# When the first weights of a fused attention and two-layer kernel are begun, and where their VectorE steps write

## Chip, cores and metric

One Trainium2 chip, one core. The metric is the device time of one execution in microseconds.

## The reference

Attention with a decay per head over blocks of 64, then a gated layer and a layer with a maximum of three, all in fp32:

```python
intra = np.einsum('bhic,bhjc->bhij', qb, kb) * Dmask[None]          # per block of 64
intra = np.einsum('bhij,bhjd->bhid', intra, vb)
inter = np.einsum('bhid,bhde->bhie', qb * lam_pow[None], kv_state)
out[:, :, sl] = intra + inter
kv_state = lam_block[None, :, None, None] * kv_state + np.einsum('bhsd,bhse->bhde', kb_dec, vb)
...
rms = np.sqrt(np.mean(x * x, axis=-1, keepdims=True) + 1e-06)       # x: 1536 x 512
xn = x / rms * rms_g
g = xn @ w_gate                                                     # d_ff 1536
silu = g * (1.0 / (1.0 + np.exp(-g)))
x = silu * (xn @ w_val) @ w_out
...
h = np.maximum(np.maximum(x @ w1, x @ w2), x @ w3)                  # d_ff 768
return h @ w_out
```

q, k and v are 2 x 8 heads x 768 x 64.

## The kernel before

Tokens are worked on as twelve tiles of 128 rows (index c), and the layers take them as three blocks of 512 (four tiles each). Each fp32 matrix product is made of three matmuls in fp32r on high and low halves (L466 to L468): a weight comes as `wh` and `wl`, an activation as `xh` and `xl`.

**Attention in rounds.** The attention of a tile is cut into pieces, named by letters in `named` (L428): T turns q and k (loads for two tiles ahead are asked for first), K makes the decayed keys `kd` on GpSimd, C the scores on TensorE, a and b mask the two halves (a also advances the state), V advances the state again, M mixes and squares, U sums the squares into `ms` and takes `ri` on GpSimd, N normalises (`x` on VectorE, `xh` on ScalarE), R makes `xl` (on GpSimd for the first eight tiles). The list `attn_q` (L430) holds the order of the pieces: round s works T on tile s, C, a, b and V on s - 1, M and U on s - 2, N and R on s - 3, and K on s + 1. Each engine runs its instructions in the order in which they are written. From tile 4 on M also reduces the squares on VectorE, so that U has one slice to sum and not four (L388 to L400).

**The seven rounds ahead of the projections** (L968) run the attention of the first tiles: rounds 0 to 6. After round 6 the first block is there, and `first_stage` begins: four steps per block, each of 24 projection matmuls (pg, then pv) and later 12 for the output, with a `gap` after every six. In the gaps of the first four steps (24 of them) the pieces of rounds 7 to 10 are placed, and in every second one `make_unit`.

**A weight** (a unit, 128 x 512) passes through stations: `load_to` asks for it on SyncE's queue (three buffers, `wraw`); `begin_unit` has ScalarE split it into words (L238, L239); `words_of_unit` has three VectorE steps (n = 0, 1, 2: L196, L199, L202) and an addition on GpSimd (L204), which also frees the `wraw` buffer; `finish_unit` casts `wh` on ScalarE (L167) and subtracts `wl` on GpSimd (L170). `make_unit` finishes the weight that has its words, does the words of the next, and begins a third. The flag `narrow` says where the middle result of the three steps lies: in the SBUF tile `W` itself while it is true, in a bank of PSUM (`mid`) when it is false. There are eight banks, which every product and every `mid` takes in turn; a new tile waits until the last reader of its bank is through.

In the seven rounds a weight is loaded at the end of each of rounds 2, 3 and 4, two at the end of rounds 5 and 6, and `make_unit` runs at the end of rounds 3 to 6. So the first weight's words are made after round 4, the second's after round 5, the third's after round 6.

Of the kernel before, what the change touches and what calls it, by code (L numbers as in the profile page):

```python
# [26 lines left out]
def tile_decay_attention_swiglu_maxout(  # L27
# [30 lines left out]
    NCH = NT // P  # L58
    CPNB = NB // P
# [35 lines left out]
    def loads_to(c):  # L95
        while nxt_load[0] <= min(c, NCH):
            n = nxt_load[0]
            if n:
                load(n - 1, 2)
            if n < NCH:  # L100
                load(n, 0)
                load(n, 1)
            nxt_load[0] += 1
# [40 lines left out]
    stage1, stage2 = [], []  # L144
# [5 lines left out]
    pos = {"load": 0, "made": 0, "raw": 0, "step": 0, "gap": 0, "quiet": False, "lag": 3, "narrow": True, "seam": False}  # L150
# [176 lines left out]
    def masked(hf):  # L327
        def piece(c):
            d = st[c]
            nc.vector.tensor_tensor(  # L330
                out=d["A"].rearrange("p (a t) i -> p t a i", t=2)[:, hf],
                in0=d["sc"][hf][:, :HF].rearrange("p (a i) -> p a i", i=C),
                in1=Tm.rearrange("p (a t) i -> p t a i", t=2)[:, hf], op=ALU.mult)
            if hf == 0:
                d["S0"] = last_state[0]
                d["S1"] = next_state(c, 0, d["S0"])
        return piece
# [40 lines left out]
    def mixed(c):  # L378
        for part in range(2):
            half_mixed(c, part)  # L380
        px = st[c]["px"]
        sq = att.tile([P, NP, P], F32, tag="sq", name="sq", bufs=1)
        x = att.tile([P, NP, P], F32, tag="x", name="x", bufs=3)
        for n in range(2):
            nc.scalar.activation(out=sq[:, 2 * n:2 * n + 2, :], in_=px[n][:, :2, :], func=AF.Square)
        for a in range(NP):
            nc.scalar.activation(out=x[:, a, :], in_=px[a // 2][:, a % 2, :], func=AF.Copy, scale=g_sb[:, a:a + 1])
        ss = sq  # L388
        if c >= CPNB:
            ss = att.tile([P, 1, P], F32, tag="ss", name="ss", bufs=1)  # L390
            nc.vector.tensor_reduce(out=ss[:, 0, :], in_=sq.rearrange("p a t -> p t a"),
                                    axis=mybir.AxisListType.X, op=ALU.add)
        st[c] = dict(x=x, ss=ss)
# [26 lines left out]
    def rest(c):  # L420
# [5 lines left out]
        eng.tensor_tensor(out=bl[:, :, ts], in0=x, in1=bh[:, :, ts].bitcast(F32), op=ALU.subtract)  # L426

    named = dict(M=(2, mixed), N=(3, normed), C=(1, scores), a=(1, masked(0)), R=(3, rest),  # L428
                 b=(1, masked(1)), U=(2, summed), V=(1, advance), T=(0, lambda c: (loads_to(c + 2), turn(c))), K=(-1, decayed_keys))
    attn_q = [(s_, named[ch][1], s_ - named[ch][0]) for s_ in range(NCH + 3)  # L430
              for ch in ("MCaNbTURVK" if s_ <= CPNB + 2 else "MNCaUbVTKR") if (ch == "K") <= s_ - named[ch][0] < NCH]
    gaps = [0, 0]

    def attn_step():
        _, fn, c = attn_q.pop(0)
        fn(c)
# [505 lines left out]
    with tc.manual_schedule():  # L942
        nc.scalar.dma_start(out=lam8, in_=lam.rearrange("(o h) -> o h", o=1).to_broadcast([P, H]))
        loads_to(0)
        for to, src in crosswise(g_sb, rms_g.rearrange("(a p) -> p a", p=P)):
            nc.scalar.dma_start(out=to, in_=src)
        make_identity(nc, ident)
        nc.vector.memset(ones, 1.0)
        nc.vector.memset(zeros, 0.0)
        nc.scalar.activation(out=mhalf, in_=zeros[:, 0:1], func=AF.Silu)  # L950
        nc.vector.memset(mhalf, -0.5)
        warm = bank("warm")
        for i in range(9):
            nc.tensor.matmul(out=warm[:, 0:P], lhsT=zeros, rhs=zeros, start=True, stop=True)
        nc.vector.tensor_tensor(out=diag, in0=ident[:, :C], in1=ident[:, C:], op=ALU.add)
        for h in range(H):
            nc.vector.tensor_tensor_scan(
                out=Tm[:, h, :], data0=lam8[:, h:h + 1].to_broadcast([P, C]), data1=diag,
                initial=0.0, op0=ALU.mult, op1=ALU.add)
        for hf in range(2):  # L960
            nc.vector.tensor_copy(out=lamh[64 * hf:64 * hf + 64, :],
                                  in_=lam8.rearrange("p (a t) -> p t a", t=2)[64 * hf:64 * hf + 64, hf, :])
        for a in range(NP):
            nc.vector.tensor_tensor_scan(
                out=lami[:, a, :], data0=lamh[:, a:a + 1].to_broadcast([P, C]), data1=zeros[:, :C],
                initial=1.0, op0=ALU.mult, op1=ALU.add)
        loads_to(1)
        for s_ in range(CPNB + 3):  # L968
            while attn_q[0][0] == s_:
                attn_step()  # L970
            load_to(pos["load"] + (0, 0, 1, 1, 1, 2, 2)[s_])
            if s_ > 2:
                make_unit()
        finish = first_stage()
        pos["step"] = len(steps)
        second_stage(finish)
# [31 lines left out]
```

## Time and profile before

| | us |
|---|---|
| median of three runs | 562.12 (561.74 to 563.1) |
| profiled execution | 560.44 |
| its span, first to last instruction | 558.6 |
| TensorE busy | 534.4 (96%) |
| VectorE busy | 385.1 (69%) |
| ScalarE busy | 279.0 (50%) |
| GpSimd busy | 317.4 (57%) |

In a timeline row stand the start, the length, the engine, the line, the operation, what is written from what, and in brackets the idle time before it with what ended it. PE is TensorE, DVE VectorE, ACT ScalarE, POOL GpSimd, SPq the DMA queue of SyncE. [...]

### The profile page before, as it was taken

To read this page: it belongs to the slowest core of one execution; us is meant where nothing else is said; L and a number is where in the kernel's file an instruction comes from. 1 tells how busy PE (TensorE), PEld (TensorE's weight loads), DVE (VectorE), ACT (ScalarE), POOL (GpSimd) and SP (SyncE) were. 2 spreads that over 40 slices of the span, in tenths; PEclk is the share of its full clock that TensorE was granted. 3 is DMA by queue.
4 is the path that set the end of the run, shared out by engine and by line. 5 is a ranking of instruction groups with operands and counts; after the bars stand their busy time and mean duration, and the time that the engine had idled before them with its cause. 6 is when DMAs were issued, how large, how long until landed. Compare 5 with 4: busy or idle time off the path is not lost.

```text
span 558.6 us, 9707 instructions
## 1 busy us (share of the span) xinstructions
PE 534.4 (96%) x3716; PEld 439.5 (79%) x3716; DVE 385.1 (69%) x664; ACT 279.0 (50%) x541; POOL 317.4 (57%) x251
## 2 busy tenths in 40 slices
PE   7976988899999999999999999999999999999997
PEld 7864766678888888888888888888888888888885
DVE  6687998363888558566685776877677577684463
ACT  3554755252474676326527445646565756551120
POOL 2366796611599668335726737787386554962050
PEclk9976989999999999999999999999999999999999
DMA  8965646200112223111312222120222322210014
GB/s 194 225 171 133 170 121 166 76 3 1 38 39 75 77 75 114 38 39 38 114 38 76 75 77 76 39 75 1 75 76 76 111 79 63 89 38 1 0 54 172
DMA packets 65453, 44.66 MB, mean 80 GB/s; under 512 B 40064, under 2 KB 61568, under 8 KB 65408
## 3 DMA queue, kind: packets, MB, share of 16 engines
q1 hardware_dynamic: 64704, 44.05, 27.5%
q8 instruction: 29, 0.48, 0.4%
q14 instruction: 16, 0.13, 0.1%
q10 hardware_dynamic: 704, 0.01, 0.1%
HBM read 40.90 MB, written 3.15 MB: 79 GB/s over the span
## 4 chain that ended last, share of the span: by engine, by line
PE 81%; POOL 7%; DVE 4%; DMA 3%; issue 2%; ACT 1%; SPq 1%; POOLq 0%; ACTq 0%; DVEq 0%
PE p L674 33%; PE r L674 8%; PE acc L466 5%; PE acc L468 5%; PE acc L467 5%; PE q L674 4%; PE acc L857 3%; PE acc L858 3%; PE acc L856 3%; POOL W L204 2%; POOL wl L170 2%; PE pv L468 2%; PE pv L466 2%; PE pv L467 1%; PE pg L467 1%
## 5 line engine op out<-in xcount | busy, mean ns | idle before, releaser
L170 POOL TENSOR_TENSOR wl<-W,wh 128x512 fp32r<-128x512 f32 x77 | 105.5, 1370 | 40.8 <-ACT wh L167 40.8
L204 POOL TENSOR_TENSOR W<-W,wraw 128x512 int32<-128x512 int32 x60 | 81.1, 1352 | 82.9 <-DVE W L202 66.2
L167 ACT CAST wh<-W 128x512 fp32r<-128x512 f32 x77 | 47.8, 621 | 92.3 <-POOL W L204 91.8
L480 POOL TENSOR_TENSOR hl<-sg,hh 128x512 fp32r<-128x512 f32 x36 | 48.3, 1341 | 33.8 <-ACT hh L479 33.8
L674 PE MATMUL p<-xh,wh 128*128 128x512 f32 x148 | 57.6, 389 | 0.0
L674 PE MATMUL p<-xl,wh 128*128 128x512 f32 x148 | 57.6, 389 | 0.0
L674 PE MATMUL p<-xh,wl 128*128 128x512 f32 x148 | 57.6, 389 | 0.0
L466 PE MATMUL acc<-hh,wh 128*128 128x512 f32 x144 | 56.6, 393 | 0.0
L467 PE MATMUL acc<-hl,wh 128*128 128x512 f32 x144 | 56.1, 389 | 0.0
L468 PE MATMUL acc<-hh,wl 128*128 128x512 f32 x144 | 56.1, 389 | 0.0
L829 DVE TENSOR_TENSOR acc_sb<-acc,acc_sb 128x512 f32<-128x512 f32 x46 | 31.8, 691 | 21.3 <-PE acc L468 20.2
L238 ACT ACTIVATE W<-wraw 128x512 f32<-128x512 f32 x60 | 40.1, 669 | 8.1 <-DMA wraw<-in_moe_w_dram 3.3
L239 ACT ACTIVATE wraw<-wraw 128x512 int32<-128x512 uint32 x60 | 39.9, 665 | 0.0
L729 ACT COPY c<-p 128x512 f32<-128x512 f32 x34 | 19.9, 586 | 38.0 <-PE p L674 37.8
L480 POOL TENSOR_TENSOR hl<-m,hh 128x512 fp32r<-128x512 f32 x18 | 24.1, 1344 | 23.0 <-ACT hh L479 22.9
L479 ACT CAST hh<-sg 128x512 fp32r<-128x512 f32 x36 | 22.3, 619 | 29.4 <-DVE sg L613 20.8
L674 PE MATMUL p<-yh,wh 128*128 128x512 f32 x90 | 35.0, 389 | 0.0
L674 PE MATMUL p<-yl,wh 128*128 128x512 f32 x90 | 35.0, 389 | 0.0
L674 PE MATMUL p<-yh,wl 128*128 128x512 f32 x90 | 35.0, 389 | 0.0
L196 DVE TENSOR_SCALAR mid<-W 128x512 f32<-128x512 f32 x46 | 31.5, 685 | 3.4 <-ACT W L238 3.4
L199 DVE TENSOR_SCALAR mid<-mid 128x512 int32<-128x512 int32 x46 | 31.9, 694 | 0.7
L674 PEld LDWEIGHTS p<-xl,wh 128*128 128x128 f32 x148 | 27.8, 188 | 5.8
(175 smaller groups left out, 1375.4 us busy)
## 6 DMA issues: line engine op xcount, KB each, us to landing
wraw<-in_moe_w_out_dram SPq DMA_DIRECT2D x18, 512.0 KB, 3.3
wraw<-in_moe_w_dram SPq DMA_DIRECT2D x18, 512.0 KB, 3.5
kn<-in_k_dram SPq DMA_DIRECT2D x12, 256.0 KB, 4.3
qn<-in_q_dram SPq DMA_DIRECT2D x12, 256.0 KB, 4.6
vn<-in_v_dram SPq DMA_DIRECT2D x12, 256.0 KB, 4.0
wraw<-in_moe_w_gate_dram SPq DMA_DIRECT2D x12, 256.0 KB, 2.9
wraw<-in_moe_w_gate_dram SPq DMA_DIRECT2D x24, 128.0 KB, 3.2
wraw<-in_moe_w_val_dram SPq DMA_DIRECT2D x12, 256.0 KB, 2.9
```

The source lines that it names most:

```text
L167: nc.scalar.copy(out=wh, in_=W.bitcast(F32))
L170: nc.gpsimd.tensor_tensor(out=wl, in0=W.bitcast(F32), in1=wh.bitcast(F32), op=ALU.subtract)
L199: nc.vector.tensor_scalar(out=mid[key], in0=mid[key], scalar1=0x07FFFFFF, scalar2=3, op0=ALU.bitwise_and, op1=ALU.logical_shift_left)
L204: nc.gpsimd.tensor_tensor(out=W, in0=W, in1=lo, op=ALU.add)
L238: nc.scalar.activation(out=W.bitcast(F32), in_=hi.bitcast(F32), func=AF.Abs)
L239: nc.scalar.activation(out=lo, in_=lo.bitcast(U32), func=AF.Copy, scale=2.0 ** -29)
L466: nc.tensor.matmul(out=out, lhsT=wh, rhs=xh_, start=first, stop=False)
L467: nc.tensor.matmul(out=out, lhsT=wh, rhs=xl_, start=False, stop=False)
L468: nc.tensor.matmul(out=out, lhsT=wl, rhs=xh_, start=False, stop=last)
L480: nc.gpsimd.tensor_tensor(out=dst_l, in0=src, in1=dst_h.bitcast(F32), op=ALU.subtract)
L674: nc.tensor.matmul(out=ps, lhsT=w[:, ks], rhs=r[:, o + k, :], start=first and k == 0 and n == 0, stop=k == 1 and n == 2, skip_group_check= ...
L829: nc.vector.tensor_tensor(out=ps if kept else y, in0=ps, in1=y, op=ALU.add)
```

## The change

The loop of the seven rounds now places the weights' steps between the attention pieces. A weight is begun at the end of each round from round 2 on, a round earlier than before. In the next round its first step stands after b, its second after U (with the finishing of the weight before it), its third, with GpSimd's addition, after V. `narrow` is false in the loop, so the middle result is a PSUM tile. One weight is asked for at the end of every round from round 0 on, seven in all as before. After the loop three weights are finished where two were, one has its words, and one is begun.

The order of the pieces changes too: in round 6 R stands right after N, ahead of U; from round 7 on it stands right after C instead of at the end. The reduction of the squares begins with tile 5 instead of tile 4.

```diff
--- before.py
+++ after.py
@@ -386,7 +386,7 @@
         for a in range(NP):
             nc.scalar.activation(out=x[:, a, :], in_=px[a // 2][:, a % 2, :], func=AF.Copy, scale=g_sb[:, a:a + 1])
         ss = sq
-        if c >= CPNB:
+        if c > CPNB:
             ss = att.tile([P, 1, P], F32, tag="ss", name="ss", bufs=1)
             nc.vector.tensor_reduce(out=ss[:, 0, :], in_=sq.rearrange("p a t -> p t a"),
                                     axis=mybir.AxisListType.X, op=ALU.add)
@@ -426,9 +426,11 @@
         eng.tensor_tensor(out=bl[:, :, ts], in0=x, in1=bh[:, :, ts].bitcast(F32), op=ALU.subtract)
 
     named = dict(M=(2, mixed), N=(3, normed), C=(1, scores), a=(1, masked(0)), R=(3, rest),
-                 b=(1, masked(1)), U=(2, summed), V=(1, advance), T=(0, lambda c: (loads_to(c + 2), turn(c))), K=(-1, decayed_keys))
-    attn_q = [(s_, named[ch][1], s_ - named[ch][0]) for s_ in range(NCH + 3)
-              for ch in ("MCaNbTURVK" if s_ <= CPNB + 2 else "MNCaUbVTKR") if (ch == "K") <= s_ - named[ch][0] < NCH]
+                 b=(1, masked(1)), U=(2, summed), V=(1, advance), T=(0, lambda c: (loads_to(c + 2), turn(c))),
+                 K=(-1, decayed_keys))
+    orders = ["MCaNbTURVK"] * (CPNB + 2) + ["MCaNRbTUVK"] + ["MNCRaUbVTK"] * NCH
+    attn_q = [(s_, named[ch][1], s_ - named[ch][0]) for s_ in range(NCH + 3) for ch in orders[s_]
+              if (ch == "K") <= s_ - named[ch][0] < NCH]
     gaps = [0, 0]
 
     def attn_step():
@@ -965,12 +967,27 @@
                 out=lami[:, a, :], data0=lamh[:, a:a + 1].to_broadcast([P, C]), data1=zeros[:, :C],
                 initial=1.0, op0=ALU.mult, op1=ALU.add)
         loads_to(1)
+        pos["narrow"] = False
+        unit_ = None
         for s_ in range(CPNB + 3):
+            if stage1:
+                unit_ = stage1.pop(0)
             while attn_q[0][0] == s_:
+                fn = attn_q[0][1]
                 attn_step()
-            load_to(pos["load"] + (0, 0, 1, 1, 1, 2, 2)[s_])
-            if s_ > 2:
-                make_unit()
+                if unit_ and fn is named["b"][1]:
+                    words_of_unit(0, *unit_)
+                elif unit_ and fn is named["U"][1]:
+                    words_of_unit(1, *unit_)
+                    if stage2:
+                        finish_unit(*stage2.pop(0))
+                elif unit_ and fn is named["V"][1]:
+                    words_of_unit(2, *unit_)
+                    stage2.append(unit_[:3])
+            load_to(pos["load"] + 1)
+            if s_ > 1:
+                begin_unit()
+        pos["narrow"] = True
         finish = first_stage()
         pos["step"] = len(steps)
         second_stage(finish)
```

## Rows read from the trace of the kernel before

**Rows 1.** Busy time by engine, four stretches; granted clock, DMA share, GB/s last.

```profile
core 0: us, PE busy (x) PEld busy (x) DVE busy (x) ACT busy (x) POOL busy (x), PEclk, DMA share, GB/s
10.00:30.00 20.00, 18.25 (x561) 16.21 (x561) 14.07 (x48) 12.28 (x34) 7.77 (x9) 1.00 0.97 227
30.00:47.70 17.70, 9.43 (x132) 7.58 (x131) 14.78 (x31) 8.99 (x22) 9.54 (x10) 0.67 0.64 164
47.70:107.70 60.00, 52.45 (x676) 39.97 (x676) 48.74 (x85) 32.41 (x70) 48.54 (x38) 0.93 0.52 138
107.70:558.60 450.90, 446.68 (x2251) 368.82 (x2251) 302.16 (x483) 221.84 (x411) 248.80 (x188) 1.00 0.19 60
```

**Rows 2.** Timeline of TensorE, 40 to 48 us: start, length, instruction, idle before.

```profile
44.27 0.80 PE L466 MATMUL pg<-xh,wh 128*128 128x512 f32 x1 [2.01 <-ACT xh L417]
47.74 0.79 PE L467 MATMUL pg<-xl,wh 128*128 128x512 f32 x1 [2.67 <-POOL xl L426]
```

**Rows 3.** Timeline of GpSimd, 37 to 47 us.

```profile
37.68 1.23 POOL L284 TENSOR_TENSOR kd<-kn,Tm 128x512 f32<-128x512 f32 x1
38.88 1.44 POOL L170 TENSOR_TENSOR wl<-W,wh 128x512 fp32r<-128x512 f32 x1
40.95 1.28 POOL L204 TENSOR_TENSOR W<-W,wraw 128x512 int32<-128x512 int32 x1 [0.63 <-DVE W L202]
45.79 0.75 POOL L404 TENSOR_TENSOR ri<-ms,mhalf 128x1 f32<-128x1 f32 x1 [3.56 <-DMA wraw<-in_moe_w_val_dram]
46.42 1.26 POOL L426 TENSOR_TENSOR xl<-x,xh 128x512 fp32r<-128x512 f32 x1
```

**Rows 4.** Timeline of VectorE, 36 to 43 us.

```profile
36.54 1.47 DVE L196 TENSOR_SCALAR W<-W 128x512 f32<-128x512 f32 x1
...
39.24 1.64 DVE L202 SCALAR_TENSOR_TENSOR W<-wraw,W 128x512 int32<-128x512 int32 x1
40.80 1.02 DVE L391 TENSOR_REDUCE ss<-sq 128x128 f32<-128x512 f32 x1
...
42.84 0.67 DVE L415 TENSOR_TENSOR x<-x,pb 128x512 f32<-128x512 f32 x1
```

**Rows 5.** Timeline of VectorE: steps of other weights, in SBUF.

```profile
28.29 1.48 DVE L196 TENSOR_SCALAR W<-W 128x512 f32<-128x512 f32 x1
...
31.00 0.69 DVE L202 SCALAR_TENSOR_TENSOR W<-wraw,W 128x512 int32<-128x512 int32 x1
...
56.61 0.43 DVE L196 TENSOR_SCALAR W<-W 128x512 f32<-128x512 f32 x1
```

**Rows 6.** Groups of VectorE by shape, 105 to 500 us: count, busy, mean ns.

```profile
L199 DVE TENSOR_SCALAR mid<-mid 128x512 int32<-128x512 int32 x45 | 31.2, 694 | 0.7
L196 DVE TENSOR_SCALAR mid<-W 128x512 f32<-128x512 f32 x45 | 30.8, 685 | 3.4 <-ACT W L238 3.4
L202 DVE SCALAR_TENSOR_TENSOR W<-wraw,mid 128x512 int32<-128x512 int32 x45 | 30.6, 680 | 0.9
```

**Rows 7.** Timeline of VectorE: qs in rounds 3, 4 and 5.

```profile
21.17 0.69 DVE L303 TENSOR_TENSOR qs<-pq,lami 128x512 f32<-128x512 f32 x1 [1.38 <-ACT qT L300]
...
26.86 0.69 DVE L303 TENSOR_TENSOR qs<-pq,lami 128x512 f32<-128x512 f32 x1 [1.95 <-ACT qT L300]
...
35.10 0.69 DVE L303 TENSOR_TENSOR qs<-pq,lami 128x512 f32<-128x512 f32 x1 [1.38 <-ACT qT L300]
```

**Rows 8.** TensorE's waits, 47.7 to 110 us: total, times, longest.

```profile
PE pg L467 <- POOL xl L426: 4.0, 2, 2.7
PE pg L468 <- POOL wl L170: 2.7, 2, 2.0
PE pv L468 <- POOL wl L170: 2.2, 2, 1.2
```

**Rows 9.** Timeline of ScalarE, 22 to 23 us.

```profile
22.53 0.67 ACT L238 ACTIVATE W<-wraw 128x512 f32<-128x512 f32 x1 [1.39 <-DMA wraw<-in_moe_w_gate_dram]
```

**Rows 10.** Timeline of SyncE's DMA issues, 42 us.

```profile
42.26 1.66 SPq L157 DMA_DIRECT2D wraw<-in_moe_w_val_dram  x3
```

## The prediction

> **What bounds the kernel now.** I first read the table by stretch [rows 1]: from 107.70 us on TensorE is busy 446.68 of 450.90 us at the full clock. That part is TensorE's own work, and the change touches little of it. Ahead of it lie two stretches with room: 30.00 to 47.70, where TensorE works 9.43 of 17.70 us at a granted clock of 0.67, and 47.70 to 107.70, with 52.45 of 60.00. So the time can move only by what moves the point 107.70, and I ask what ends last in each of the two.
>
> The first stretch is round 6, the last of the seven rounds ahead of the projections. TensorE's timeline [rows 2] shows its end: the first projection matmul waits for xh until 44.27, the second waits for xl until 47.74. VectorE's [rows 4] shows why xh is late: ahead of round 6 the three steps of the second weight run from 36.54 to 40.80 (4.26 us), a reduction of squares takes 1.02, and only then come a mask, a state and x at 42.84. GpSimd's [rows 3] shows why xl is later still: it starts at 46.42, behind ri at 45.79, which reads nothing but the mean square (the load that the row names as its releaser is no input of it); xh was there by 44.27.
>
> The second stretch I read from TensorE's waits [rows 8]: 2.7 + 2.2 = 4.9 us for the low half of a weight (wl), and 4.0 for xl, of which 2.67 is the one of [rows 2], so 1.3 is at the stretch's end. GpSimd, which makes wl and xl, is busy 48.54 of 60.00 [rows 1]: loaded, but not full.
>
> **The start of the projections, part by part.** The edit has five parts that reach it.
>
> (1) In round 6 the step R (xl of block 0's last tile) now stands ahead of ri. Its start moves from 46.42 to where xh is ready, 44.27 [rows 2, 3]: 2.15 us off. ri comes 1.3 us later in its place; nobody waits for it until the next round's normalisation.
>
> (2) The tile of index 4 keeps no reduction: 1.02 us off VectorE [rows 4]. TensorE then sums four slices instead of one. It was idle for 2.01 us right there [rows 2], so that is free.
>
> (3) The three steps of a weight go through a PSUM bank. The same steps do so later in this kernel, at 0.685, 0.694 and 0.680 us, 2.06 in all [rows 6]. Of the two weights made in the rounds now, the first one's steps run from 28.29, the last of them starts at 31.00 and holds the engine for some 0.6 [rows 5], 3.3 us together; the second's take 4.26 [rows 4]. Savings: 1.25 and 2.2.
>
> (4) A third weight is now ahead of x in round 6 (weights 0, 1 and 2 instead of 0 and 1): 2.06 more. But the steps are spread: each weight's first step stands after the second mask, where VectorE waits for ScalarE's qT, 1.38, 1.95 and 1.38 us in rounds 3 to 5 [rows 7]. The first steps of three weights, 0.685 each, fit in there: 2.06 off. Net nothing; without that cover it costs 2.06.
>
> (5) In GpSimd's queue the third weight's addition and the next tile's decayed keys now come right ahead of xl: 1.28 + 1.23 = 2.5 us [rows 3]. They run beside x and xh, which take 1.4 us, from 42.84 to 44.27 [rows 2, 4]; 1.2 of it I count as hidden. I take 1.3 back, with 0 and 2.5 as ends.
>
> A wait that the trace of before does not show is the PSUM bank itself: a round takes nine of the eight banks now, so some TensorE or VectorE step can wait for the last step on the bank. It costs at least nothing; at most the third step's 0.68 in each of three rounds, 2.0. Of the eight banks a round used so far TensorE's rows show no such wait in rounds 3 to 5, so I take 0.6, nearer to the low end.
>
> Sum: 2.15 + 1.0 + 1.25 + 2.2 + 0 = 6.6 off, 1.3 + 0.6 back: 4.7 us. The projections start at 43.0 instead of 47.7. Ends: 6.6 - 2.5 - 2.0 = 2.1 and 6.6.
>
> [...] What the rows show: with GpSimd idle the first step takes 0.43 us in SBUF (at 56.61, [rows 5]), in PSUM 0.685 [rows 6]; with GpSimd at work it takes 1.48 [rows 5] and 1.47 [rows 4]. [...] Both weights of the rounds met a busy GpSimd, so I go by the rows 4 and 5.
>
> Loads: one weight is asked for in each round from round 0, two more before round 5 than now. At 227 GB/s, with the transfer engines 0.97 busy from 10 to 30 us [rows 1], 512 KB takes 2.3 us; the q, k and v behind them come up to 4.6 us later. Rounds are 5.7 us apart and then 8.2 [rows 7], and later the transfers were ahead of the rounds: the queue issues the fifth weight only at 42.26, after waiting for GpSimd to free its buffer [rows 10]. That slack covers the 4.6. If it did not, the rounds would be later by as much. On the other side ScalarE stood for 1.39 us for the first weight's load after round 3 [rows 9]; a load two rounds earlier ends that. I count neither.
>
> **The stretch to 107.70.** On entry one more weight is finished, and one more is begun. A weight is advanced at every second gap, and the stretch has 24 gaps in 60 us: two are 5.0 us. The longest wait for wl is 2.0 [rows 8], so all 4.9 us of them go if GpSimd follows. The 1.3 us for xl at the end go as well, since R stands ahead of ri and of the next keys in rounds 7 to 10. What may be late next is GpSimd: a weight's addition and its wl, 1.28 and 1.44 [rows 3], are now done before the stretch, which leaves 45.8 us of the 48.54; in a stretch of some 54 us that is 85%, as against 81% before. I take 1.0 back, between 0 and 4. In rounds 7 to 10 xl now may stand in the queue waiting for xh (0.8 us each, what lies between x's end and 44.27 [rows 2, 4]), which is within those ends; for later rounds R is VectorE's, with 302.16 us of 450.90 busy, and costs nothing. Sum: 6.2 - 1.0 = 5.2 us; ends 2.2 and, if 1.5 us of slow clock goes too (0.93 there), 7.7.
>
> **Sum.** 4.7 + 5.2 = 9.9 us off the profiled execution's 560.44, which is 550.5. That execution lies 1.7 under the median of the three runs, 562.12, so the median to expect is 552.2. The ends, 2.1 + 2.2 and 6.6 + 7.7, give 557.8 and 547.8.
>
> **Rivals.**
> - GpSimd becomes the bound of the stretch: it is at 81%, in a queue that runs in order. The start moves by 4.7, the rest stays: 557.4. For it: wl and xl are all that TensorE waits for [rows 8]. Against: 11.5 us of its 60 were idle.
> - The early weight loads delay q, k and v by the whole 4.6 us, and the start stays; the stretch still gains: 556.9. Against it are the 8.2 us between rounds 4 and 5 [rows 7], where the loads were not what was late.
> - Both of these: what is saved is lost again, 561.7, no change.
> [...]
> - More goes: start at 41.1, all the waits, slow clock too: 547.
> - Slower: TensorE's clock falls to its lower level in round 4 already. In the rows it is full at 18.25 of 20.00 us busy and 0.67 at 9.43 of 17.70 [rows 1]. With a weight's steps in each, rounds last some 6.3 us; TensorE has 5.2 of work in a round of 5.7. At the lower level that is 10.4, 4 more than 6.3, in three rounds (3 to 5; round 6 ran slow already): 12 us. The start is then 55.0 instead of 43.0, so 7.4 later than now, and the stretch gives 5.2 back: 564.3. It decides once the clock falls before round 4; after that it costs one round or less and lies within the forecast's ends.
>
> **How the numbers follow.** Forecast 552.2 (547.8 to 557.8): 0.55. GpSimd as the bound, 557.4: 0.13. Loads late, 556.9: 0.07. Rule on the bank, 557.2: 0.03. More goes, 547: 0.07. Both, 561.7: 0.06. Slow clock, 564.3: 0.09. A measurement of this kernel tells 0.3% (1.7 us) from no change. Faster: 0.55 + 0.13 + 0.07 + 0.03 + 0.07 = 0.85; same 0.06; slower 0.09. From 546.5 to 559.0 lie all cases but the last two and about a tenth of the forecast's, which fills the 8 in 10.
>
> **What would show it.** In the profile after: the first matmul that reads xl near 43 us; xl ahead of ri on GpSimd in round 6; the three steps near 0.69 each in rounds 3 to 6, and no idle time of VectorE ahead of qs there; no reduction in round 6; waits of TensorE for wl under 1 us in sum up to its second block, and that block's start near 98 us. Wrong would be: a granted clock under 1.00 before 25 us, TensorE's matmuls of a round waiting for L202, or ScalarE's first step of a weight waiting for a load for over 2 us. If xl starts on GpSimd long after xh is done, term (5) was too small; if waits for wl remain, GpSimd has become the bound.

## The result and the profile after

| | before | changed |
|---|---|---|
| median | 561.99 us (561.74 to 563.1) | 547.97 us (547.22 to 550.31) |
| ratio | | 0.9754 [0.972, 0.9788] |
| profiled execution, its span | 560.44, 558.6 | 550.31, 548.5 |
| the same kernel once more: median | 560.99 | 547.51 (546.98 to 548.09) |
| ratio; profiled execution, span | | 0.9758 [0.9735, 0.978]; 547.79, 546.0 |

The changed kernel is 14.0 us faster; the prediction was 9.9 us. The 547.97 lies inside the range of 547.8 to 557.8, at its very end; the same kernel once more, 547.51, lies just below it. (The forecast went out from 562.12, the median of three of the four runs of before.) The profiled execution of the first set was the longest of its four, so a second profile, of a typical execution, stands beside it all through ("the repeat").

I measure every kernel at two points: the first projection matmul that reads xl ("the start", 47.74 before [rows 2]) and the first one of the second block ("block 1", 107.72 before). Between them lies "the stretch". From block 1 on all kernels here take 450.3 to 450.9 us but one, so the rest of the document is about these two points.

| | start | block 1 | stretch |
|---|---|---|---|
| before | 47.74 | 107.72 | 59.98 |
| changed, first profile | 44.76 | 98.12 | 53.36 |
| changed, repeat | 41.13 | 95.63 | 54.50 |

Busy times of the repeat ahead of its start and in its stretch, in the columns of [rows 1]:

```profile
30.00:41.10 11.10, 7.52 (x147) 6.12 (x145) 9.45 (x29) 8.45 (x21) 10.26 (x11) 0.96 0.84 202
41.10:95.60 54.50, 51.32 (x676) 41.05 (x677) 42.95 (x81) 30.21 (x67) 46.01 (x37) 0.91 0.60 156
```

In the stretch TensorE is idle for 3.2 us of 54.5; before it was idle for 7.55 of 60.0. Before the start GpSimd is now the fullest engine, 10.26 of 11.10. The start itself, on TensorE, GpSimd, VectorE and once more TensorE of the repeat (it answers to [rows 2], [rows 3] and [rows 4, 7]):

```profile
38.90 0.50 PE L468 MATMUL pg<-xh,wh 128*128 128x512 f32 x1 [1.02 <-ACT xh L417]
41.13 0.79 PE L469 MATMUL pg<-xl,wh 128*128 128x512 f32 x1 [1.73 <-POOL xl L426]
```

```profile
37.55 1.29 POOL L204 TENSOR_TENSOR W<-W,wraw 128x512 int32<-128x512 int32 x1
38.80 1.06 POOL L284 TENSOR_TENSOR kd<-kn,Tm 128x512 f32<-128x512 f32 x1
39.81 1.27 POOL L426 TENSOR_TENSOR xl<-x,xh 128x512 fp32r<-128x512 f32 x1
41.05 0.54 POOL L404 TENSOR_TENSOR ri<-ms,mhalf 128x1 f32<-128x1 f32 x1
```

```profile
32.27 0.68 DVE L196 TENSOR_SCALAR mid<-W 128x512 f32<-128x512 f32 x1
33.73 0.69 DVE L303 TENSOR_TENSOR qs<-pq,lami 128x512 f32<-128x512 f32 x1 [0.78 <-ACT qT L300]
...
34.40 0.69 DVE L199 TENSOR_SCALAR mid<-mid 128x512 int32<-128x512 int32 x1
...
35.76 0.68 DVE L202 SCALAR_TENSOR_TENSOR W<-wraw,mid 128x512 int32<-128x512 int32 x1
...
37.46 0.68 DVE L415 TENSOR_TENSOR x<-x,pb 128x512 f32<-128x512 f32 x1
```

```profile
29.77 0.66 PE L294 MATMUL pk<-ident,kn 128*128 128x128 f32 x4 [0.25 <-DVE S L348]
```

xl is ahead of ri on GpSimd, the three steps take 0.68 to 0.69 us each, the reduction is gone. No matmul waits for L202. But the turning of k (the last row) waits for L348, VectorE's state, which it does not read: L348 frees a bank of scores. That is a wait for a PSUM bank, 0.25 and 0.24 us in two rounds (29.77 and 35.90). All kernels here with the middle result in a bank in the rounds show it but the one with one weight less alone, and none of the others does. And xl still stands behind the weight's addition and the keys: it starts at 39.81, 0.9 us after TensorE had xh. qs, the scaled q of a tile that VectorE makes once a round, recurs every 6.12 us (21.48, 27.60, 33.73, 39.85), with VectorE full but for 0.78 us a round.

TensorE's waits from 41 us to 100 us, the repeat (line, what it waited for, total, times, longest); the 1.7 is the one at the start:

```profile
PE sc L318 <- ACT x L387: 2.3, 2, 2.2
PE pg L469 <- POOL xl L426: 1.7, 1, 1.7
PE px L374 <- DVE S L348: 0.4, 1, 0.4
```

Against [rows 8] the 4.9 us for wl are gone, as is the 1.3 for xl at the stretch's end; 2.3 for the scores' x is new.

What made the first profile 2.5 us longer than the repeat stands ahead of the start. TensorE stood twice inside a tile's scores, with no releaser ("issue": it waited for nothing that the profile shows); then its clock fell. Timeline of TensorE and stretches of the first profile:

```profile
18.60 0.34 PE L323 MATMUL sc<-vn,kd 64*64 64x64 f32 x8 [1.24 <-issue]
...
25.92 0.69 PE L323 MATMUL sc<-vn,kd 64*64 64x64 f32 x29 [2.62 <-issue]
```

```profile
23.00:26.00 3.00, 0.38 (x24) 0.25 (x18) 2.21 (x8) 2.17 (x8) 2.51 (x3) 1.00 1.00 266
...
30.00:34.00 4.00, 3.89 (x129) 3.59 (x126) 2.86 (x9) 3.45 (x10) 3.03 (x4) 0.50 0.98 234
```

After 3 us in which TensorE was busy for 0.38 the granted clock (third column from the right, 1.00 is full speed) fell from 1.00 to 0.50, its lower level: no stretch here shows less. The 32 score matmuls of L318 took 1.08 us there (at 31.87), and 0.69 at the full clock (at 22.51). In the repeat the same two stalls took 0.61 and 1.00 us and the clock stayed at 1.00 until 40 us. They are taken up again in the last section.

### The profile page after: what moved, and what is told of

Same layout as the page of the kernel before. It is cut to its first block, busy times and chain, and to the rows that moved or that the text cites. A ratio compares the mean times of both kernels' runs of the same rounds, so it can differ in the third digit from the quotient of the medians.

```text
span 548.5 us, 9716 instructions
## 1 busy us (share of the span) xinstructions
PE 529.8 (97%) x3722; PEld 438.9 (80%) x3722; DVE 376.5 (69%) x663; ACT 278.6 (51%) x541; POOL 316.3 (58%) x251
## 4 chain that ended last, share of the span: by engine, by line
PE 85%; POOL 4%; issue 3%; DVE 3%; SPq 2%; ACT 2%; DMA 1%; POOLq 0%; ACTq 0%
PE p L676 34%; PE r L676 8%; PE acc L468 6%; PE acc L470 6%; PE acc L469 6%; PE q L676 4%; PE acc L859 3%; PE acc L858 3%; PE acc L860 3%; PE pv L468 2%; PE pv L469 2%; PE pv L470 2%; PE pg L468 2%; SPq L92 2%; PE pg L470 2%
## 5 line engine op out<-in xcount | busy, mean ns | idle before, releaser
L482 POOL TENSOR_TENSOR hl<-m,hh 128x512 fp32r<-128x512 f32 x18 | 24.0, 1343 | 23.0 <-ACT hh L481 22.9
L196 DVE TENSOR_SCALAR mid<-W 128x512 f32<-128x512 f32 x50 | 34.2, 685 | 3.0 <-ACT W L238 3.0
L199 DVE TENSOR_SCALAR mid<-mid 128x512 int32<-128x512 int32 x50 | 34.7, 694 | 0.7
L202 DVE SCALAR_TENSOR_TENSOR W<-wraw,mid 128x512 int32<-128x512 int32 x50 | 34.0, 680 | 1.0
```

The lines of the kernel that those rows point to most:

```text
L196: nc.vector.tensor_scalar(out=mid[key].bitcast(F32), in0=W.bitcast(F32), scalar1=LEAST, scalar2=MOST, op0=ALU.max, op1=ALU.min)
L199: nc.vector.tensor_scalar(out=mid[key], in0=mid[key], scalar1=0x07FFFFFF, scalar2=3, op0=ALU.bitwise_and, op1=ALU.logical_shift_left)
L482: nc.gpsimd.tensor_tensor(out=dst_l, in0=src, in1=dst_h.bitcast(F32), op=ALU.subtract)
```

## The experiments

Each "start" and "block 1" below is from one profiled execution, and the two profiles of the changed kernel alone differ by 3.6 us at the start. So verdicts go by the medians, and the profile says where.

**The changed kernel once more**, beside experiments that share its runs of before.

> The changed kernel once more, as the yardstick of the three beside it. The profile shown has 550.31 us and a TensorE clock of 0.991, the other runs 547.2 to 548.7 and 0.994 to 0.997. Theory: the spread is the clock in rounds 4 and 5; where TensorE stands 2.6 us in the scores of round 4 the clock falls to its lower level for some 7 us, in other executions later or not. Then this run's profile, if it is one of the fast ones, has no stretch at 0.50 between 26 and 34 us, and the first block's end is 2 to 3 us earlier. Rival: the spread lies elsewhere in the span; then the first 98 us are alike. Time 548, within 0.3%.

Measured: 547.51 us, the numbers above. The theory holds: from 26 to 34 us this profile has a clock of 1.00, and block 1 comes 2.5 us earlier.

**The order alone.** The kernel before with the new order of the pieces and the reduction from tile 5 on.

```diff
-        if c >= CPNB:
+        if c > CPNB:
-              for ch in ("MCaNbTURVK" if s_ <= CPNB + 2 else "MNCaUbVTKR") if (ch == "K") <= s_ - named[ch][0] < NCH]
+              for ch in ("MCaNbTURVK" if s_ <= CPNB + 1 else "MCaNRbTUVK" if s_ == CPNB + 2 else "MNCRaUbVTK") if (ch == "K") <= s_ - named[ch][0] < NCH]
```

> The kernel before with only the order of the pieces changed (R ahead of ri in round 6, right after C from round 7; the reduction from tile 5 on); weights, their places and loads as before. Theory: xl no longer waits behind ri (2.15 us) and the reduction of 1.02 us goes from the path, so the first matmul that reads xl comes 2 to 3 us earlier, and the 1.3 us wait for xl at the end of the first block goes: 3 to 4.5 us in all, 556.5 to 558. Rival: VectorE and GpSimd are late from the weights' steps in SBUF anyway, the start moves by less than 1 us, 560 to 561.

Measured: 554.41 us, ratio 0.9869 [0.985, 0.9888]: 7.3 us off, more than either expectation. Start 45.22, block 1 102.22. TensorE's start, and VectorE's way to it:

```profile
43.86 0.79 PE L466 MATMUL pg<-xh,wh 128*128 128x512 f32 x1 [3.13 <-ACT xh L417]
45.22 0.80 PE L467 MATMUL pg<-xl,wh 128*128 128x512 f32 x1 [0.56 <-POOL xl L426]
```

```profile
35.64 0.69 DVE L303 TENSOR_TENSOR qs<-pq,lami 128x512 f32<-128x512 f32 x1 [1.38 <-ACT qT L300]
...
42.43 0.68 DVE L415 TENSOR_TENSOR x<-x,pb 128x512 f32<-128x512 f32 x1
```

The wait for xl falls from 2.67 [rows 2] to 0.56, as term (1) has it. From qs to x VectorE takes 6.79 us, where it took 7.74 before (35.10 to 42.84, [rows 4, 7]): the reduction's 0.95. 4.3 us of waits for wl remain.

**The loop alone.** The changed kernel with the old order and the old reduction.

```diff
-        if c > CPNB:
+        if c >= CPNB:
-    orders = ["MCaNbTURVK"] * (CPNB + 2) + ["MCaNRbTUVK"] + ["MNCRaUbVTK"] * NCH
+    orders = ["MCaNbTURVK"] * (CPNB + 3) + ["MNCaUbVTKR"] * NCH
```

> The changed kernel with the old order of the pieces and the reduction from tile 4 on: the loop of the rounds is the only thing changed. Theory (the parts add): what the order alone gives is missing, 3 to 4.5 us, so 550.5 to 552 us; xl stands behind ri in round 6 again and the reduction of 1.0 us ahead of x. Rival (the order only works with the loop, or the loop makes room that hides it): as fast as the changed kernel within 1.5 us, 547 to 549.

Measured: 554.07 us, ratio 0.9875 [0.9854, 0.9897]: 7.6 us off, less than either expectation. The medians' gains, 7.3 and 7.6, add to a little more than the whole of the change (14.9 against 13.5 to 14.0). Start 47.06, block 1 103.60 (in an execution of 556.35, 2.3 over the median). TensorE and GpSimd at its start:

```profile
42.29 0.79 PE L468 MATMUL pg<-xh,wh 128*128 128x512 f32 x1 [2.02 <-ACT xh L417]
47.06 0.79 PE L469 MATMUL pg<-xl,wh 128*128 128x512 f32 x1 [3.98 <-POOL xl L426]
```

```profile
43.82 0.55 POOL L404 TENSOR_TENSOR ri<-ms,mhalf 128x1 f32<-128x1 f32 x1 [1.53 <-DVE ms L402]
44.33 1.27 POOL L170 TENSOR_TENSOR wl<-W,wh 128x512 fp32r<-128x512 f32 x1
45.56 1.45 POOL L426 TENSOR_TENSOR xl<-x,xh 128x512 fp32r<-128x512 f32 x1
```

xh is there 2.0 us earlier than before, but xl is behind ri and now behind a wl too, since the loop finishes a weight after U. The loop shows its gain at the start only when R stands ahead of U. In the stretch, 56.54 us here, no wait for wl is left even in the old order.

**The later order alone.** The kernel before, R right after C from round 7 on, nothing else.

```diff
-              for ch in ("MCaNbTURVK" if s_ <= CPNB + 2 else "MNCaUbVTKR") if (ch == "K") <= s_ - named[ch][0] < NCH]
+              for ch in ("MCaNbTURVK" if s_ <= CPNB + 2 else "MNCRaUbVTK") if (ch == "K") <= s_ - named[ch][0] < NCH]
```

> The kernel before with the new order only from round 7 on (R right after C); round 6, the reduction, the weights and loads as before. The order as a whole gave 7.3 us, where 4.5 had been worked out: 2.15 and 1.0 in round 6, 1.3 at the first block's end. Theory (the later order is worth more than the wait at the block's end, since xl ahead of ri, V, T and the keys also moves GpSimd's weights up): 3.5 to 5 us, 557 to 558.5, with the start at 47.7 as before. Rival (the excess lies in round 6: the half-rate stretch behind it gets shorter): 1 to 1.8 us, 560 to 561.

Measured: 555.99 us, ratio 0.991 [0.9892, 0.9928]: 5.2 us off, a little more than the theory gives. Start 49.16 (1.4 later than before, though nothing ahead of it is changed), block 1 104.08: the stretch is 54.92, near the change's 54.50, with the weights made as before. TensorE's longest wait for wl in it, and the stretch:

```profile
PE pg L468 <- POOL wl L170: 2.5, 1, 2.5
```

```profile
49.16:104.08 54.92, 50.83 (x677) 39.57 (x678) 44.26 (x84) 31.38 (x69) 48.21 (x38) 0.95 0.57 151
```

TensorE is idle for 4.09 us of it, 3.45 less than before, and busy for 1.6 us less at a clock of 0.95 for 0.93. Where the idle time was shows on TensorE and GpSimd of the kernel before, in the last of the four steps:

```profile
94.21 0.50 PE L468 MATMUL pg<-xh,wl 128*128 128x512 f32 x1 [0.64 <-POOL wl L170]
...
99.78 0.50 PE L468 MATMUL pv<-xh,wl 128*128 128x512 f32 x1 [1.24 <-POOL wl L170]
...
107.72 0.50 PE L467 MATMUL pg<-xl,wh 128*128 128x512 f32 x1 [1.28 <-POOL xl L426]
```

```profile
94.13 1.29 POOL L204 TENSOR_TENSOR W<-W,wraw 128x512 int32<-128x512 int32 x1
95.39 1.24 POOL L284 TENSOR_TENSOR kd<-kn,Tm 128x512 f32<-128x512 f32 x1
96.58 1.47 POOL L426 TENSOR_TENSOR xl<-x,xh 128x512 fp32r<-128x512 f32 x1
98.02 1.71 POOL L170 TENSOR_TENSOR wl<-W,wh 128x512 fp32r<-128x512 f32 x1
```

K and R stood together at the end of a round's list, and the wl of the second of these waits (98.02) stood behind both. The xl of the third stood behind K; the wl of the first did not stand behind either. With R moved apart none of the three waits is left but 0.2 us. The longest wait for wl, in an earlier step, is not cured by this move: 2.04 us before (at 76.11), the 2.5 above here. The order alone, which has this move too, shows a stretch of 57.00 from an earlier start (45.22), so one stretch by itself is no price; the medians are, 5.2 us for this move and 7.3 for the whole order.

**The middle result in SBUF.** The changed kernel with `narrow` left true in the loop.

```diff
-        pos["narrow"] = False
```

> As the changed kernel, but the three VectorE steps in the seven rounds keep their middle result in SBUF as before. Theory (the bank spares VectorE the contention with GpSimd): a step that runs beside GpSimd takes 1.2 to 1.5 us in place of 0.69, the third 1.6; two or three of the twelve steps of four weights meet it, so that the projections start 1 to 4 us later, 549 to 552 us. Rival (in the new places GpSimd is idle when the steps run: it waits for ms ahead of the second step, and runs only from the third on): the first and second steps take 0.43 and the kernel is as fast as the changed one or 0.5 us faster.

Measured: 549.83 us, ratio 0.9799 [0.9777, 0.9821], 2.3 us more than the repeat; start 42.46. VectorE, a weight's steps:

```profile
32.87 0.71 DVE L196 TENSOR_SCALAR W<-W 128x512 f32<-128x512 f32 x1
...
34.99 0.42 DVE L199 TENSOR_SCALAR W<-W 128x512 int32<-128x512 int32 x1
...
36.09 1.51 DVE L202 SCALAR_TENSOR_TENSOR W<-wraw,W 128x512 int32<-128x512 int32 x1
```

2.64 us for this weight (2.33 for the first one, 2.65 for the second) against 2.06 through the bank, and rounds of 6.69 instead of 6.12. In their new places the first two steps are quick in SBUF too (0.71 and 0.42, where the first took 1.47 in its old place [rows 4] and the second, in the kernel of the order alone, 1.16); only the third is slow. There GpSimd subtracts a wl (35.79 to 37.05). With W and wraw in SBUF the step takes 1.51 beside that subtraction; with the bank as one input it takes 0.68 beside the same one (35.76 in the repeat, the subtraction from 35.08 to 36.36). In the kernel before, with both inputs in SBUF, it took 0.69 at 31.00 [rows 5], where GpSimd was idle from 30.68 to 31.77, and 1.64 at 39.24 [rows 4], beside the wl of 38.88 [rows 3].

**One weight less ahead**, the loads as changed.

```diff
-            if s_ > 1:
+            if s_ > 2:
```

> As the changed kernel, but a weight is begun at the end of each round only from the fourth round on, so that the rounds make one weight less (as far ahead as in the kernel before). Theory (one weight more on entry is what takes TensorE's waits for wl): the waits for wl of 3 to 5 us in sum come back in the first block, 551 to 553 us. Rival (they went because the start of the projections and GpSimd's queue changed): under 1.5 us of them come back, within 0.3% of the changed kernel, and the projections start 1 us or more earlier, since GpSimd and VectorE have one weight less ahead of xl.

Measured: 550.61 us, ratio 0.981 [0.9784, 0.9835], 3.1 us more than the repeat. It looks like the price of a weight, and a wait of 2.4 us for wl is back in the stretch. But TensorE and SyncE's queue (of the shortest execution, 548.46, 2.15 below the median) show another wait, ahead of the start:

```profile
36.99 0.99 PE L323 MATMUL sc<-vn,kd 64*64 64x64 f32 x16 [3.29 <-DMA vn<-in_v_dram]
```

```profile
30.90 1.68 SPq L157 DMA_DIRECT2D wraw<-in_moe_w_gate_dram  x3
32.67 0.54 SPq L92 DMA_DIRECT2D vn<-in_v_dram  x1
```

With the weights a round later, the fourth weight's load waits for its buffer until 30.90, and the v of a tile stands behind it in the queue: TensorE waits 3.29 us for v.

**One weight less, its loads out of the way.**

```diff
-            load_to(pos["load"] + 1)
-            if s_ > 1:
+            load_to(pos["load"] + (0, 1, 1, 1, 1, 1, 2)[s_])
+            if s_ > 2:
```

> One weight less ahead, as in the run with one weight less, but the loads begin in round 1, so that the fourth weight's load, which has to wait for a buffer, stands behind the v of tile 5 in the DMA queue and not ahead of it (there v came late and TensorE stood 3.29 us in round 6). Theory (of the 3 us that the run with one less lost, about half was that queue and half the wait of 2.44 us for wl that came back): the 3.29 us go, the start of the projections comes to 39.5 to 40.5, the wait for wl stays, 548 to 549.5. Rival (the start is set by the rounds' own period and the queue only hid it): 550 to 551, start at 41 to 42. Another: without the weight in the rounds all is as fast as the changed kernel, 547.5, and the weight ahead was worth nothing.

Measured: 546.83 us (546.28 to 547.87), ratio 0.9747 [0.973, 0.9764]: nothing lost, the last of the three expectations. Start 40.05, stretch 54.53. So with the new order the weight ahead brings no time. It exchanges one wait for another; first TensorE with one weight less, then TensorE and ScalarE of the repeat:

```profile
67.73 0.50 PE L470 MATMUL pg<-xh,wl 128*128 128x512 f32 x1 [2.43 <-POOL wl L170]
```

```profile
72.89 0.32 PE L318 MATMUL sc<-qT,kT 64*64 64x64 f32 x2 [2.15 <-ACT x L387]
...
70.04 0.62 ACT L167 CAST wh<-W 128x512 fp32r<-128x512 f32 x1 [3.01 <-POOL W L204]
```

In the repeat no wl is late, but ScalarE stands for 3.01 us for GpSimd's addition, and the mixing of a tile, queued behind it on ScalarE, comes late to TensorE, which waits 2.15 us for it. Either way what is waited for is a result of GpSimd.

**The loads a round later**, the weights as changed.

```diff
-            load_to(pos["load"] + 1)
+            load_to(pos["load"] + (0, 1, 1, 1, 1, 1, 2)[s_])
```

> As the changed kernel, but no weight is asked for in round 0: the first in round 1, then one a round, two in round 6. Theory (TensorE's two stalls in the scores, 1.24 us at 17.4 and 2.62 at 23.3, which the profile gives to no engine, are the engine waiting for its next block of instructions, and that block waits behind the weights and tiles in the transfer engines): with 512 KB less in the way at that point both shrink towards the 0.33 and 0.22 of the kernel before, the clock stays full up to 30 us and the projections start 1 to 3 us earlier, 545 to 547 us. Rival (the stalls are waits for a tile's v or k that comes late): they shrink as well, but then the stall ends when that tile lands; the landing times in the trace tell. Against both: the first weight now comes later than ScalarE begins it, 1 to 2 us of idle ScalarE in round 3.

Measured: 549.52 us, ratio 0.9798 [0.9775, 0.9822], 2.0 more than the repeat; start 42.56, 1.4 later. TensorE's first stall did shrink, to 0.33 us, and the second is gone, as the theory has it; but the time did not follow. ScalarE, whose first step of a weight waits:

```profile
18.56 0.68 ACT L238 ACTIVATE W<-wraw 128x512 f32<-128x512 f32 x1 [3.85 <-DMA wraw<-in_moe_w_gate_dram]
```

The second weight's first step waits for 1.88 (at 24.72). TensorE was busy for 2.07 of the 4 us from 18 to 22, and its granted clock was 0.65 in the next 4. The loads of this kernel are those of the one before it, with one weight less: there the weights are begun a round later too, ScalarE's first steps wait for no load, and the time is 546.83. So asking in round 0 is what the early weights need, and no gain by itself.

**Four warming matmuls fewer**, which moves every later TensorE instruction forward in its stream.

```diff
-        for i in range(9):
+        for i in range(5):
```

> The changed kernel with five warming matmuls at the start instead of nine: 4 fewer, so each later instruction of TensorE stands some 8 matmul rows earlier in its stream; nothing else differs. The two stalls without a releaser stand after 24 of 32 rows of the second group of scores in round 3 and after 3 of 32 in round 4, in each run so far of this order. Theory (TensorE waits for a block of instructions): both stalls move back by some 8 rows, to after 32 and after 11 or so, wherever the data are. Rival (a tile's or weight's data are late): they stay after 24 and 3. Time: the start is not later; 547 to 549, or 1 to 3 us more if the clock is not up at the first round.

Measured: 547.0 us, ratio 0.9744 [0.9725, 0.9764], the repeat's time. What it did to the stalls stands in the last section.

**The keys behind xl**, in round 6.

```diff
-                 K=(-1, decayed_keys))
-    orders = ["MCaNbTURVK"] * (CPNB + 2) + ["MCaNRbTUVK"] + ["MNCRaUbVTK"] * NCH
+                 K=(-1, decayed_keys), k=(0, decayed_keys))
+    orders = ["MCaNbTURVK"] * (CPNB + 1) + ["MCaNbTURV", "MCaNRkbTUVK"] + ["MNCRaUbVTK"] * NCH
```

> The changed kernel with one GpSimd step moved: the decayed keys of tile 6 stand after xl in round 6 instead of ahead of it. Theory (the queue of GpSimd sets the start: in the yardstick's profile TensorE waits 1.73 us for xl after xh): xl comes 1.0 to 1.2 us earlier, TensorE's wait for it falls to some 0.6, and the whole gains 0.5 to 1.2 us, 546.3 to 547. Rival (the start is given back in the first block, where GpSimd has no room): the start moves by 1 us and the first block's end by less than 0.3 us, 547.5.

Measured: 547.41 us, ratio 0.9753 [0.9735, 0.977]. TensorE's wait for xl falls from 1.73 to 0.84 and the start comes to 40.34; the stretch is 54.64. TensorE waits 1.9 us in it for a state, 0.8 for x and 0.7 more for a sum, where the repeat has 0.4 for a state and 2.3 for x. The time stays, as the rival has it, but the reason given there is not shown: in the profile (547.15, the shortest of its five) block 1 is at 94.98, so 0.65 of the 0.79 us that the start gained are still there, where the rival gives less than 0.3.

**More sums on TensorE**: no VectorE reduction before tile 8.

```diff
-        if c > CPNB:
+        if c >= 2 * CPNB:
```

> The changed kernel with the reduction of squares left out for tiles 5, 6 and 7 as well (TensorE sums four slices for them). Theory (VectorE is what ends late in the first block, busy 22.8 of 25 us from 47 to 72): 3 times 1.05 us go from it, TensorE gets 3 times 0.7 more; the block ends 0.5 to 2 us earlier, 545.5 to 547. Rival (TensorE pays and GpSimd is the bound, 22.6 of the same 25): 547.5 to 549.

Measured: 549.29 us, ratio 0.9788 [0.9772, 0.9805], 1.8 more than the repeat. Block 1 at 95.39 is 0.2 us earlier than the repeat's, and so is the last matmul of all (541.82 for 542.02); the profiled execution ended 1.0 later, so this profile doesn't show what the median lost. The run took no work off VectorE. From 47 to 72 us it has three steps fewer and the same busy time as the repeat, 22.75 us (the third busy time; the repeat's row stands under the next experiment):

```profile
47.00:72.00 25.00, 24.13 (x340) 19.28 (x338) 22.75 (x39) 16.18 (x35) 22.27 (x18) 1.00 0.47 133
```

```profile
L196 DVE TENSOR_SCALAR W<-W 128x512 f32<-128x512 f32 x8 | 8.6, 1070 | 0.0
```

The weights' steps, in SBUF again after the seven rounds, took longer: the eight first steps of this stretch 1070 ns each (second row; 678 in the repeat). So whether VectorE holds the stretch stays open. No run kept these steps in the bank after the seven rounds, the change that would tell.

**Three at once**: one weight less with free loads, the keys behind xl, five warming matmuls.

```diff
-        for i in range(9):
+        for i in range(5):
-            load_to(pos["load"] + 1)
-            if s_ > 1:
+            load_to(pos["load"] + (0, 1, 1, 1, 1, 1, 2)[s_])
+            if s_ > 2:
```

The diff of the keys is the one above.

> Three edits of earlier runs at once: one weight less ahead with its load out of the way, the keys of tile 6 behind xl in round 6, and five warming matmuls for nine. Alone they stood 0.7, 0.1 and 0.5 us below the repeat of the changed kernel (547.51). Theory A, they lie in different places and add: 546.2 us, the first matmul with xl near 39.5 and block 1 near 94. Theory B, GpSimd and VectorE, each some 90% busy between 47 and 72 us, set the end of the stretch, and what the start gains is given back there, as with the keys alone: 546.8 to 547.5, block 1 at 94.6 or later. All have 450.4 from block 1 to the end.

Measured: 547.41 us, ratio 0.975 [0.9732, 0.9768]. The start, 39.79, is the earliest of all. Of the 1.3 us that it lies ahead of the repeat's, 0.9 are left at block 1 (94.77); against one weight less alone, 0.3 us ahead at the start, block 1 is 0.2 later. Stretches from 47 to 72 us, the repeat and this kernel:

```profile
47.00:72.00 25.00, 23.15 (x330) 18.28 (x328) 22.75 (x42) 16.44 (x36) 22.63 (x19) 1.00 0.49 131
```

```profile
47.00:72.00 25.00, 22.15 (x325) 17.40 (x324) 23.03 (x43) 16.81 (x37) 23.13 (x18) 1.00 0.49 134
```

GpSimd goes from 22.63 to 23.13 us of 25 and TensorE from 23.15 to 22.15. Theory B holds by the time and by block 1: the three gains do not add. That GpSimd and VectorE set the end is read from their shares and was not tested. None of these variants can be told from the changed kernel, so there is no better version to show.

## Why the prediction was right, and where it was not

The sum was 9.9 us off the profiled execution; the repeat's is 12.65 off (560.44 to 547.79): 6.6 at the start (forecast 4.7), 5.5 in the stretch (5.2), 0.5 after it. The rest, up to the 14.0 of the medians, is that the profiled execution of before lay 1.55 under its median and the repeat's only 0.2 under the changed kernel's, where the forecast gave both the same offset.

**The start.**
- (1) R ahead of ri, 2.15: right. The order alone cuts the wait for xl from 2.67 to 0.56.
- (2) The reduction, 1.02: right, 0.95 from qs to x in the kernel of the order alone, and TensorE's four sums cost nothing that shows. No run changed it by itself.
- (3) The bank, 1.25 and 2.2: the sum was right, its cause mostly not. The forecast put both down to PSUM, by steps in SBUF of 1.47 and 1.48 us [rows 4, 5]. Kept in SBUF in the new places a weight takes 2.64 us; so the places brought the old 3.3 and 4.26 down to 2.64, and the bank took the last 0.58 (0.27 for the first weight): 0.83 less on the third step, 0.27 more on the second. The median puts the bank at 2.3 us over all weights of the rounds. The failed step is putting the whole of the old durations down to SBUF, without asking whether GpSimd would be at work beside the steps in their new places. The places' share is read from the durations; no run has the bank in the old places.
- (4) The third weight, net nothing: right. The rounds are 6.12 us for the 6.3 assumed. That no idle time would stay ahead of qs was wrong: 0.78 us a round stays.
- (5) GpSimd's queue, 1.3 back: right in kind, a little large. xl starts 0.9 us after xh was there; the keys' experiment takes that 0.9 back.
- The bank as a wait, 0.6: 0.49 in two rounds, so right, though taken out of a range of 0 to 2.0 with no row behind it. It falls on the turning of k behind a state, not on the third step.
- The loads, counted at nothing: the largest miss, but one inside the change. With the weights begun a round earlier and no early loads ScalarE waits 3.85 and 1.88 us, and the median is 2.0 us more. The row was there: ScalarE's 1.39 [rows 9], and 1.31 more for the second weight (28.13 before); with weights a round earlier these waits had to grow. With weights and loads both a round later the time is the same as with both early, so asking in round 0 is a condition of the early weights, and no gain by itself.

With the measured values: 2.1 + 0.95 + 3.45 - 0.9 - 0.5 = 5.1. The repeat shows 6.6, although its stalls take 1.3 us more than the 0.33 of before (0.61 + 1.00 - 0.33). So 1.5 to 2.8 us of the start have no term; the end of ScalarE's two waits for loads, 2.7 us before, is the nearest row, and no run takes it apart. A single start is also uncertain: 1.4 us later with nothing changed ahead of it, in the later order alone.

**The stretch.** Right in size (block 1 was to start near 98 us: 98.12 in the first profile, 95.63 in the repeat); but the causes overlap, where the forecast added them. It gave 4.9 us to one weight more ahead, and 1.3 to R's move for the one xl at the end. The loop alone does end all waits for wl, as worked out, and its stretch is 3.4 us shorter. But the order alone takes off 3.0, the later order 5.1 (by medians 5.2 of the 14.0), and both edits together 5.5: in the last step a wl stood behind K and R on GpSimd, and either moving R or an earlier weight ends that wait. With the order in place, one weight less ahead costs nothing (54.53). So the step that failed is "all 4.9 us of them go": they go, but a wait of 2.3 us for x, by way of ScalarE, comes for the last 2.6 of them. GpSimd is 84% busy there (46.01 of 54.50), as against 85% in the forecast; the 1.0 us back that the forecast took for it was too little for that wait. That the sum came out is in part luck: the 4.9 us were credited to the weight ahead, which brings nothing once the order is there.

**The rivals.** GpSimd as the bound of the stretch was given 557.4, for no gain there at all. That did not happen. It may decide what comes next: the keys and the three at once gain nothing by their medians, though their profiles keep 0.65 of 0.79 and 0.9 of 1.3 us at block 1. Loads late: the opposite. The one mechanism of it that does exist was seen with one weight less, where a load that waits for its buffer holds up v for 3.29 us. The rule on the bank, 557.2: that steps in PSUM cost more than they save is the author's estimate, and no run shows it. A weight took 2.06 us through the bank and 2.33 to 2.65 in SBUF in the same places; the second step alone was dearer in the bank each time, by 0.27 us (0.69 against 0.42), the first step only for the first weight (0.68 against 0.41), and the third saved 0.83. Slow clock in round 4: it did come in the first profile, from 27 us on, by a cause that the prediction had not named; that execution was 2.5 us longer than the repeat, not 12. The doubling of TensorE's work that the 12 us take is nearly what the trace of before shows: projection matmuls of 128x512 follow each other at 0.43 us at a clock of 0.50 (48.33 to 49.61) and at 0.23 at 1.00 (111.07 to 112.00). Three times of the rivals are off by their own sums, and no chance hangs on it: 6.6 + 7.7 off gives 547.8 for the case that more goes, not 547; a start at 55.0 is 7.3 later, not 7.4; and with neither part saved the time is 562.1, not 561.7.

## What to carry to other kernels

The steps that were slow beside GpSimd had two remedies here, another memory (the third step, 1.51 us in SBUF, 0.68 through the bank) and another place in the order (the first step, 1.47 in its old place, 0.71 in its new one), and only a run that changes one of them tells which did it; a sum that comes out right proves neither. Where an engine works through one queue for several readers, look at what the late result stands behind before making more of it ahead. Before a wait in the trace is counted at nothing, work out how it grows when the step that waits comes earlier.

## What the runs showed of the hardware

TensorE stalled here with no releaser at fixed places of its instruction stream, for 0.31 to 2.62 us at a time. In most of these kernels they fall after 24 of the 32 matmuls of L323 in round 3, and after 3 of 32 in round 4: 125 matmuls apart, each with its weight load, so 250 instructions. In four kernels one more falls after 14 or 15 of the 32 of L318 in round 5, another 125 or 126 on. TensorE of the repeat, then of the kernel with one weight less (18 of 32 are still to come):

```profile
17.60 0.34 PE L323 MATMUL sc<-vn,kd 64*64 64x64 f32 x8 [0.61 <-issue]
...
23.29 0.69 PE L323 MATMUL sc<-vn,kd 64*64 64x64 f32 x29 [1.00 <-issue]
```

```profile
28.51 0.50 PE L318 MATMUL sc<-qT,kT 64*64 64x64 f32 x18 [1.25 <-issue]
```

Two kernels have four warming matmuls fewer, which are eight in the trace (10 for 18). Theirs, the three at once and then the four fewer alone:

```profile
23.05 0.57 PE L323 MATMUL sc<-vn,kd 64*64 64x64 f32 x21 [0.54 <-issue]
...
28.05 0.39 PE L318 MATMUL sc<-qT,kT 64*64 64x64 f32 x10 [0.31 <-issue]
```

```profile
28.24 0.35 PE L318 MATMUL sc<-qT,kT 64*64 64x64 f32 x9 [0.31 <-issue]
```

Here the breaks fall after 11 of 32 and after 22 or 23: eight matmuls later in the program, as many as were taken out ahead. With the four fewer alone only the last of the breaks took any time. So the breaks belong to a count of instructions and not to the data. The profile lists a queue that brings instructions:

```profile
q8 instruction: 29, 0.48, 0.4%
```

That is 29 packets in 0.48 MB, some 16.5 KB each, before and after. The table counts their time on the 16 transfer engines, which are 0.97 busy from 10 to 30 us before [rows 1]. Before, one of these packets starts between 14.6 and 14.7 us, and the break in round 3 ends at 17.29; in the first profile of the changed kernel they start between 16.1 and 16.3 and between 22.9 and 23.0, and the breaks end at 18.60 and 25.92. So these three breaks end 2.3 to 3.0 us after a packet starts. That TensorE waits there for its instructions is the author's inference from the count and these times; no run changed that queue by itself. The breaks took 0.33 us in the kernel before and up to 2.62 in the changed one, with a fall of the clock behind it. What sets the length stays open: in round 3 it was 0.33 with the loads a round later, but 0.85 and 0.91 with the old loads and the later order.

The end has a scatter of its own: from the end of the last addition on VectorE to the end of the span the repeat took 2.9 us and the kernel with more sums on TensorE 4.1, for the same last store.
